# Seven products of halves for x w1 and x w2 of the last two chunk indices, in an RWKV and multiplicative feed-forward kernel

## The chip, the core and the metric

The kernel runs on one core of a Trainium2 chip. The metric is the device time of one launch in microseconds (us). Four runs of the kernel before gave a median of 510.1 us (509.72 to 511.49).

The core has engines that each run their own list of instructions in order and wait for each other by semaphores: PE (matmuls, with weight loads beside them), DVE (vector), ACT (scalar, mostly copies here), POOL (used only in the setup) and SP, which issues the DMA transfers. Matmul results land in PSUM[...]. ACT and DVE carry them on to SBUF.

## What is computed

```python
def _attn_ref(r, k, v, w, u):             # B, H, S, D = 4, 8, 768, 48
    state = zeros((B, H, D, D))
    for t in range(S):
        cur = einsum('bhd,bhe->bhde', u[None] * kt, vt)
        y[:, :, t] = einsum('bhd,bhde->bhe', rt, state + cur)
        state = w[None, :, :, None] * state + einsum('bhd,bhe->bhde', kt, vt)
...
x = attn_out.transpose(0, 2, 1, 3).reshape(B * S, H * D)      # 3072 x 384
a = x @ w1                                # 384 x 1024
b = x @ w2
h = a * b @ w3                            # 1024 x 1024
return h @ w_out                          # 1024 x 384
```

All of it is fp32. The kernel multiplies w3 by w_out first, so that the end is (a * b) times one matrix of 1024 x 384, which it calls w34.

## The kernel before

**Visits.** The sequence is cut into 6 chunks of 128 steps, and a visit is one chunk of one batch row, so there are 24 visits, n = 4c + b. A visit makes a 128-column part of `xT[c]`, the transposed x of chunk index c (384 rows in three blocks of 128, by 512 tokens of the four batch rows). Four visits complete one `xT[c]`.

**The order is written out by hand.** `ORDER` is a list of words such as `a.2.3.2`, and `listed()` runs the function of each word in turn. Each engine gets its instructions in the order of the words. A word says nothing of waits: those follow from the buffers. The words that matter here, with their lines:

- a visit: `kk`, `rr`, `v` load k, r and v (L200); `k` scales k and r on DVE (L404); `x` transposes blocks on DVE (L473); `y` writes them to a scratch in DRAM (L477) and `z` reads them back into one of two buffers `tt` (L485), both on SP; `l` copies the k half on ACT (L490); `d`, `e`, `f`, `g` make the diagonal (L413 to L431); `U` (L517) and `A` (L524) are the state and pair products on PE, `i`, `j` (L540, L541) and `m` (L552) take them on DVE; `o`, `p` spread the state on ACT (L549); `S` (L624) and `V` (L638) make the visit's output on PE, and `Y` (L646) copies it into `xT` on ACT. There is one PSUM buffer for U and A, and one for S and V. Visit n+2 uses the same `tt` as visit n, so `z` of visit n+2 waits for S of visit n.
- the wide products: `a.c.j.part` is x w1 for chunk index c and the 128 columns j of w1, as three matmuls of 128x512 (one for each block of 128 rows of x), L664. `c` copies it to SBUF on ACT (L670), `b` is the same with w2, and `u` multiplies both on DVE into `abt[c, j]` (L675). They share two PSUM banks (tag `f`).
- the last product: `s` makes sums of quarters of `abt` (L708, L711, DVE); `P.c.m.x` is one of seven products of halves, four matmuls of 128x192 (L721); `E` gathers them (L736 on ACT, L738 to L750 on DVE); `D` stores 128 rows of the output (L754). They use the same two banks `f`.
- the weights: `W` fetches (L219), `M`, `N`, `H`, `L`, `Q` convert (L354 to L369), and `G`, `K`, `F`, `X` make w34.

Before the change the words a, c, b, u run for all six chunk indices. The words for c = 4 begin between visits 20 to 23, and those for c = 5 come after visit 23; P, E and D of c = 4 and 5 are interleaved with them.

Of the kernel before, what the change touches and what calls it, by code (L numbers as in the profile page):

```python
# [8 lines left out]
F32 = mybir.dt.float32  # L9
# [13 lines left out]
kk.2 rr.2 v.2 d.0 W.2 N.0 e.0 f.0 M.0 k.0 g.0 H.0 U.0 kk.3 rr.3 d.1 T.0 k.1 L.0 R.0 e.1 kk.4 rr.4 t.0 i.0 f.1 r.0 T.1  # L23
W.3 Q.0 p.0 A.0 M.1 h.1 j.0 S.0 t.1 d.2 R.1 k.2 m.0 r.1 R.2 kk.5 rr.5 e.2 U.1 N.1 r.2 f.2 A.1 M.2 H.1 T.2 i.1 L.1 m.1
V.0 d.3 p.1 W.4 Q.1 v.3 Y.0 t.2 j.1 S.1 g.2 N.2 A.2 k.3 V.1 H.2 R.3 kk.6 rr.6 Y.1 U.2 m.2 M.3 v.4 T.3 N.3 L.2 a.0.0.0
k.4 r.3 W.5 i.2 a.0.1.0 H.3 p.2 c.0.0.0 e.3 L.3 R.4 j.2 S.2 f.3 M.4 W.6 U.3 Q.3 b.0.0.0 o.4 h.3 c.0.1.0 i.3 t.3 V.2
d.4 p.3 k.5 kk.7 rr.7 T.4 Y.2 e.4 A.3 v.5 r.4 x.5 S.3 t.4 b.0.1.0 m.3 o.5 y.5 j.3 M.5 V.3 u.0.0.0 u.0.1.0 U.4 f.4 Y.3
v.6 A.4 Q.2 g.4 a.0.0.1 k.6 N.5 b.0.0.1 M.6 N.6 m.4 c.0.0.1 H.6 a.0.1.1 z.5 u.0.0.1 L.6 H.5 b.0.1.1 c.0.1.1 x.6 W.9
L.5 a.0.2.2 u.0.1.1 y.6 i.4 W.8 l.5 Q.6 p.4 d.5 a.0.3.2 Q.5 c.0.2.2 kk.8 rr.8 j.4 N.4 e.5 S.4 H.4 c.0.3.2 M.8 z.6 U.5
f.5 M.9 V.4 N.8 d.6 L.4 A.5 i.5 kk.9 rr.9 b.0.2.2 Y.4 h.5 o.6 e.6 W.7 p.5 m.5 v.7 l.6 Q.4 b.0.3.2 j.5 u.0.2.2 N.9 k.7  # L30
U.6 f.6 A.6 x.7 g.6 S.5 k.8 y.7 V.5 d.7 M.7 a.0.4.2 m.6 v.8 kk.10 rr.10 o.7 e.7 u.0.3.2 Y.5 f.7 z.7 x.8 b.0.4.2
c.0.4.2 d.8 y.8 h.7 kk.11 rr.11 e.8 i.6 a.0.5.2 f.8 p.6 u.0.4.2 l.7 d.9 j.6 b.0.5.2 c.0.5.2 e.9 H.8 f.9 L.8 H.9 W.11
d.10 L.9 A.7 Q.8 W.12 U.7 u.0.5.2 a.0.6.2 N.7 i.7 H.7 p.7 k.9 L.7 a.0.7.2 j.7 kk.12 rr.12 c.0.6.2 x.9 W.10 Q.9 y.9 S.6
Q.7 c.0.7.2 z.8 o.8 V.6 m.7 e.10 b.0.6.2 Y.6 g.8 v.9 N.10 N.11 S.7 M.10 f.10 M.11 u.0.6.2 z.9 V.7 o.9 H.10 b.0.7.2 l.8
d.11 Y.7 H.11 v.10 L.10 e.11 L.11 Q.10 W.13 g.9 Q.11 W.14 a.1.0.2 N.12 u.0.7.2 M.12 f.11 H.12 M.13 a.1.1.2 d.12 L.12
N.13 e.12 c.1.0.2 W.15 Q.12 M.14 H.13 N.14 L.13 b.1.0.2 H.14 c.1.1.2 W.16 Q.13 L.14 Q.14 W.17 M.15 N.15 b.1.1.2 H.15
u.1.0.2 L.15 Q.15 W.18 M.16 N.16 A.8 H.16 u.1.1.2 a.1.2.2 L.16 m.8 l.9 W.19 N.17 M.17 Q.16 H.17 M.18 b.1.2.2 N.18
c.1.2.2 H.18 L.17 L.18 Q.17 W.20 M.19 Q.18 W.21 G.0.0 N.19 G.0.1 K.0.0 u.1.2.2 U.8 H.19 a.1.3.2 K.0.1 i.8 L.19 k.10
p.8 W.22 M.20 N.20 kk.13 rr.13 x.10 F.0 c.1.3.2 H.20 M.21 y.10 j.8 L.20 Q.19 W.23 M.22 Q.20 N.21 N.22 H.21 H.22 L.21
b.1.3.2 X.0 Q.21 W.24 L.22 Q.22 W.25 M.23 N.23 A.9 u.1.3.2 U.9 H.23 S.8 i.9 L.23 z.10 V.8 k.11 o.10 a.1.4.2 g.10 N.24  # L40
x.11 v.11 kk.14 rr.14 Q.23 Y.8 m.9 y.11 b.1.4.2 p.9 W.26 N.25 f.12 c.1.4.2 j.9 l.10 d.13 e.13 S.9 u.1.4.2 o.11 A.10
z.11 a.1.5.2 m.10 a.1.6.2 c.1.5.2 l.11 a.1.7.2 c.1.6.2 b.1.5.2 V.9 u.1.5.2 U.10 c.1.7.2 v.12 G.1.0 i.10 Y.9 G.1.1 g.11
k.12 b.1.6.2 x.12 kk.15 rr.15 p.10 f.13 y.12 K.1.0 d.14 b.1.7.2 M.24 j.10 M.25 e.14 u.1.6.2 K.1.1 H.24 S.10 H.25 L.24
z.12 A.11 u.1.7.2 o.12 U.11 Q.24 L.25 V.10 m.11 W.28 G.2.0 k.13 g.12 W.27 G.2.1 v.13 F.1 i.11 kk.16 rr.16 Q.25 p.11
f.14 N.26 Y.10 j.11 l.12 d.15 K.2.0 x.13 K.2.1 e.15 y.13 N.27 G.3.0 X.1 U.12 S.11 k.14 o.13 V.11 i.12 kk.17 rr.17 A.12
Y.11 x.14 G.3.1 v.14 g.13 a.2.0.2 z.13 m.12 K.3.0 f.15 y.14 p.12 d.16 G.4.0 K.3.1 e.16 b.2.0.2 j.12 K.4.0 c.2.0.2 l.13
U.13 u.2.0.2 S.12 k.15 z.14 o.14 V.12 i.13 A.13 Y.12 x.15 G.4.1 g.14 v.15 F.2 m.13 y.15 kk.18 rr.18 K.4.1 f.16 l.14
d.17 M.26 e.17 M.27 H.26 p.13 H.27 L.26 j.13 S.13 L.27 W.29 Q.26 M.28 W.30 V.13 Q.27 o.15 z.15 N.28 A.14 Y.13 H.28
U.14 X.2 m.14 G.5.0 L.28 v.16 G.5.1 i.14 g.15 F.3 W.31 Q.28 N.29 k.16 M.29 f.17 kk.19 rr.19 p.14 H.29 j.14 L.29 x.16
l.15 Q.29 S.14 y.16 K.5.0 N.30 d.18 X.3 F.4 K.5.1 N.31 e.18 o.16 z.16 G.6.0 X.4 G.6.1 K.6.0 F.5 M.30 K.6.1 H.30 M.31  # L50
L.30 H.31 Q.30 L.31 s.1.2.0 Q.31 s.1.2.1 F.6 s.1.0.0 X.5 s.1.2.3 s.1.1.0 s.1.3.0 s.1.1.2 s.1.3.1 s.1.1.1 s.1.3.3
s.1.3.2 s.1.0.1 s.1.0.2 s.1.0.3 s.1.2.2 G.7.0 X.6 s.1.1.3 U.15 K.7.0 G.7.1 i.15 P.0.0.0 K.7.1 k.17 p.15 F.7 x.17 kk.20
rr.20 j.15 y.17 A.15 X.7 s.0.1.0 V.14 s.0.0.0 E.0.0.0 l.16 B.0 P.0.1.0 Y.14 v.17 s.0.0.1 g.16 m.15 a.2.1.2 s.0.0.3 B.1
E.0.1.0 f.18 B.2 a.2.2.2 c.2.1.2 B.3 s.0.1.2 s.0.0.2 s.0.2.0 b.2.1.2 d.19 c.2.2.2 s.0.2.2 s.0.2.1 s.0.1.1 s.0.2.3
s.0.3.0 b.2.2.2 s.0.1.3 s.0.3.1 u.2.1.2 s.0.3.3 e.19 s.0.3.2 P.0.0.2 u.2.2.2 P.0.1.2 E.0.0.2 P.0.0.3 E.0.1.2 P.0.0.4
E.0.0.3 P.0.1.3 E.0.0.4 P.0.0.5 E.0.1.3 P.0.1.5 E.0.0.6 E.0.0.5 D.0.0.0 P.0.1.4 E.0.1.6 A.16 E.0.1.4 U.16 E.0.1.5 m.16
D.0.1.0 P.0.0.6 i.16 k.18 p.16 P.0.0.1 j.16 kk.21 rr.21 S.15 x.18 z.17 o.17 V.15 E.0.0.1 E.0.0.7 U.17 Y.15 a.2.3.2
i.17 g.17 y.18 v.18 k.19 D.0.0.1 kk.22 rr.22 p.17 f.19 a.2.4.2 l.17 d.20 j.17 c.2.3.2 x.19 e.20 y.19 P.0.1.1 c.2.4.2
P.0.1.6 E.0.1.1 P.1.0.0 E.0.1.7 D.0.1.1 P.1.0.2 E.1.0.0 P.1.0.3 E.1.0.2 P.1.0.4 E.1.0.3 P.1.0.5 E.1.0.4 P.1.1.0
E.1.0.6 E.1.0.5 D.1.0.0 P.1.0.1 E.1.1.0 P.1.0.6 E.1.0.1 P.1.1.1 E.1.0.7 D.1.0.1 P.1.1.2 E.1.1.1 P.1.1.3 E.1.1.2  # L60
P.1.1.4 E.1.1.3 b.2.3.2 E.1.1.4 b.2.4.2 u.2.3.2 P.2.0.0 u.2.4.2 s.2.0.0 P.1.1.5 s.2.0.2 E.2.0.0 s.2.0.1 s.2.0.3
P.2.1.0 E.1.1.5 E.1.1.6 D.1.1.0 P.1.1.6 A.17 E.1.1.7 S.16 D.1.1.1 E.2.1.0 m.17 z.18 o.18 V.16 U.18 g.18 a.2.5.2 i.18
v.19 k.20 p.18 f.20 kk.23 rr.23 x.20 l.18 a.2.6.2 c.2.5.2 j.18 y.20 d.21 e.21 b.2.5.2 c.2.6.2 a.2.7.2 u.2.5.2 s.2.1.0
s.2.1.2 s.2.1.1 s.2.1.3 b.2.6.2 c.2.7.2 b.2.7.2 u.2.6.2 s.2.2.0 s.2.2.1 s.2.2.2 s.2.2.3 a.3.0.2 Y.16 u.2.7.2 s.2.3.0
s.2.3.1 s.2.3.2 s.2.3.3 b.3.0.2 c.3.0.2 P.2.1.2 u.3.0.2 P.2.0.1 E.2.1.2 P.2.0.2 E.2.0.1 P.2.0.3 E.2.0.2 P.2.0.4
E.2.0.3 P.2.0.5 E.2.0.4 P.2.0.6 E.2.0.5 E.2.0.6 D.2.0.0 P.2.1.3 E.2.0.7 D.2.0.1 P.2.1.4 E.2.1.3 P.2.1.5 E.2.1.4
P.2.1.1 E.2.1.5 E.2.1.6 D.2.1.0 a.3.1.2 E.2.1.1 b.3.1.2 c.3.1.2 P.2.1.6 u.3.1.2 a.3.2.2 E.2.1.7 D.2.1.1 b.3.2.2
c.3.2.2 S.17 u.3.2.2 z.19 o.19 V.17 A.18 Y.17 a.3.3.2 g.19 m.18 v.20 l.19 f.21 b.3.3.2 d.22 c.3.3.2 e.22 A.19 u.3.3.2
U.19 m.19 S.18 i.19 z.20 o.20 V.18 k.21 p.19 a.3.4.2 x.21 g.20 v.21 j.19 y.21 Y.18 P.3.0.0 f.22 l.20 d.23 c.3.4.2 U.20
e.23 E.3.0.0 A.20 i.20 b.3.4.2 k.22 p.20 m.20 x.22 U.21 a.3.5.2 u.3.4.2 y.22 k.23 s.3.0.0 s.3.0.2 s.3.0.1 b.3.5.2  # L70
# [22 lines left out]
def kernel(  # L93
    ctx: ExitStack,
    tc: tile.TileContext,
    r: bass.AP,
    k: bass.AP,
    v: bass.AP,
    w: bass.AP,
    u: bass.AP,  # L100
    moe_w1: bass.AP,
    moe_w2: bass.AP,
    moe_w3: bass.AP,
    moe_w_out: bass.AP,
    out: bass.AP,
):

# [28 lines left out]
    Q = 32  # L147
# [740 lines left out]
```

## Time and profile before

One execution was profiled. It took 513.74 us, its span in the trace is 512.0 us, and 1.7 us lie around the span.

| engine | busy, us | share of the span | instructions |
|---|---|---|---|
| PE (matmul) | 494.3 | 97% | 5222 |
| PE weight loads, beside the matmuls | 325.5 | 64% | 5222 |
| DVE | 277.8 | 54% | 587 |
| ACT | 183.0 | 36% | 456 |
| POOL | 6.0 | 1% | 23 |

The profile's views used below are: the busy times of each engine, for the span or for stretches of it (windows); groups of instructions with busy time, mean time of one, and the idle time before them with what ended it; the waits of one engine; the chain of work that ended last; and the timeline. An fp32 matmul stands in the trace as two instructions, one after the other, so the 138 + 138 matmuls of 128x512 at L664 are counted as 276 + 276. "Mean ns of one" includes what overlaps with the next matmul; the busy time divided by the count is what one adds to PE.

### The profile page before, as it was taken

Reading aid. Unit: us, or ns where it says so; the run is one execution under the profiler, and the core shown is the slowest. Engines: PE = TensorE matmul, PEld = TensorE weight load, DVE = VectorE, ACT = ScalarE, POOL = GpSimd, SP = SyncE. Lnnn points to the kernel's source line nnn. Section 1 sums busy time; section 2 is a strip of 40 time slices with the busy share of each in tenths; the row PEclk is TensorE's granted clock in tenths of the full one; section 3 lists DMA queues with packets and bytes.
Section 4 is the critical chain, followed back from the end, with each engine's and each line's share of the span. In section 5 each row is a group of like instructions: output and inputs, shape, how many; then the busy total and the mean of one; then the engine's idle time right before and its main releaser. Section 6 shows DMA issues by size and latency. Waiting matters only on the chain.

```text
span 512.0 us, 12255 instructions
## 1 busy us (share of the span) xinstructions
PE 494.3 (97%) x5222; PEld 325.5 (64%) x5222; DVE 277.8 (54%) x587; ACT 183.0 (36%) x456; POOL 6.0 (1%) x23
## 2 busy tenths in 40 slices
PE   5689999999999999999999999999999999999996
PEld 5577555355466766678887487564965654855486
DVE  6989998789286767756325432285322215221342
ACT  4676556576277764303103200341061410001000
POOL 4000000000000000000000000000000000000000
PEclk8889999999999999999999999999999999999999
DMA  8898886668448680304402201230060100000001
GB/s 206 192 235 244 237 214 194 180 222 247 130 110 229 172 231 13 78 0 118 116 32 76 65 0 47 63 109 2 1 167 4 49 1 1 15 15 17 1 18 66
DMA packets 96864, 52.72 MB, mean 103 GB/s; under 512 B 77729, under 2 KB 88225, under 8 KB 96801
## 3 DMA queue, kind: packets, MB, share of 16 engines
q1 hardware_dynamic: 96592, 51.85, 37.0%
q8 instruction: 43, 0.70, 0.6%
q14 instruction: 21, 0.16, 0.1%
q10 hardware_dynamic: 208, 0.00, 0.0%
HBM read 39.65 MB, written 12.19 MB: 101 GB/s over the span
## 4 chain that ended last, share of the span: by engine, by line
PE 85%; DMA 6%; DVE 4%; SPq 2%; ACT 1%; issue 1%; ACTq 0%; DVEq 0%
PE ps_b L664 22%; PE ps_a L664 21%; PE ps_w L392 7%; PE ps_y L624 3%; PE ps_y L638 3%; PE ps_s4b L721 3%; PE ps_a12b L721 3%; PE ps_a22t L721 3%; PE ps_s2t L721 3%; PE ps_s1t L721 3%; PE ps_s3t L721 3%; PE ps_a11b L721 3%; PE ps_a L524 3%; PE ps_a L517 2%; DMA raw<-in_moe_w_dram 2%; DMA tt<-scratch 1%
## 5 line engine op out<-in xcount | busy, mean ns | idle before, releaser
L664 PE MATMUL ps_b<-xT,w 128*128 128x512 f32 (+1 forms) x300 | 131.1, 578 | 1.2 <-ACT a L670 1.1
L664 PE MATMUL ps_a<-xT,w 128*128 128x512 f32 (+1 forms) x300 | 131.4, 581 | 0.0
L664 PEld LDWEIGHTS ps_b<-xT,w 128*128 128x128 f32 x300 | 56.0, 190 | 63.9 <-issue 56.7
L675 DVE TENSOR_TENSOR abt<-ps_b,a 128x512 f32<-128x512 f32 (+1 forms) x50 | 33.3, 667 | 111.3 <-PE ps_b L664 111.3
L664 PEld LDWEIGHTS ps_a<-xT,w 128*128 128x128 f32 x300 | 55.3, 190 | 56.9 <-issue 53.6
L670 ACT COPY a<-ps_a 128x512 f32<-128x512 f32 (+1 forms) x50 | 28.2, 567 | 129.3 <-PE ps_a L664 125.4
L549 ACT COPY wide<-st 64x192 f32<-64x192 f32 x88 | 30.6, 348 | 56.0 <-PE ps_y L624 28.1
L431 ACT ACTIVATE AT<-same,dg 128x64 f32<-128x64 f32 x160 | 40.4, 335 | 6.4 <-DVE dg L420 3.9
L392 PE MATMUL ps_w<-wo,w3T 128*128 128x384 f32 x128 | 42.5, 487 | 0.0
L392 PEld LDWEIGHTS ps_w<-wo,w3T 128*128 128x128 f32 x128 | 23.9, 190 | 15.7 <-ACT wide L549 0.2
L366 ACT ACTIVATE t<-raw 128x512 uint32<-128x512 uint32 (+2 forms) x32 | 22.5, 708 | 7.5 <-DVE w3n L362 4.9
L624 PEld LDWEIGHTS ps_y<-tt,wide 128*32 128x32 f32 x1056 | 15.9, 110 | 11.6 <-issue 8.4
L404 DVE TENSOR_TENSOR krs<-krin,pn_in 128x768 f32<-128x768 f32 x24 | 22.7, 948 | 0.0
L624 PE MATMUL ps_y<-tt,wide 128*32 128x64 f32 x1056 | 19.7, 221 | 2.8 <-ACT xT L646 2.8
L638 PE MATMUL ps_y<-AT,vnat 64*64 64x64 f32 x1152 | 22.4, 223 | 0.0
L517 PE MATMUL ps_a<-vnat,krs 64*64 64x48 f32 x704 | 16.7, 227 | 5.8 <-DVE krs L404 4.1
L638 PEld LDWEIGHTS ps_y<-AT,vnat 64*64 64x64 f32 x1152 | 19.3, 136 | 3.0 <-issue 1.3
L552 DVE COPY_PREDICATED AT<-later,ps_a 128x512 f32<-128x512 int32 x24 | 17.4, 726 | 6.8 <-PE ps_a L524 3.7
L473 DVE STREAM_TRANSPOSE tr<-krs 128x768 f32<-128x768 f32 x19 | 18.5, 973 | 4.5 <-DMA scratch<-tr 4.3
L517 PEld LDWEIGHTS ps_a<-vnat,krs 64*64 64x64 f32 x704 | 14.4, 142 | 9.8 <-issue 9.4
L490 ACT COPY kT<-tt 128x512 f32<-128x512 f32 x19 | 11.7, 618 | 20.8 <-DMA tt<-scratch 19.7
L359 DVE TENSOR_SCALAR t<-raw 128x512 uint32<-128x512 uint32 (+2 forms) x32 | 13.9, 437 | 9.4 <-DMA raw<-in_moe_w_dram 5.0
(108 smaller groups left out, 572.3 us busy)
## 6 DMA issues: line engine op xcount, KB each, us to landing
raw<-in_moe_w_dram SPq DMA_DIRECT2D x16, 512.0 KB, 5.0
scratch<-tr SPq DMA_DIRECT2D x19, 384.0 KB, 3.6
raw<-in_moe_w_dram SPq DMA_DIRECT2D x8, 768.0 KB, 6.3
tt<-scratch SPq DMA_DIRECT2D x38, 128.0 KB, 3.2
krin<-in_k_dram SPq DMA_DIRECT2D x24, 192.0 KB, 4.1
krin<-in_r_dram SPq DMA_DIRECT2D x24, 192.0 KB, 4.4
vnat<-in_v_dram SPq DMA_DIRECT2D x24, 192.0 KB, 4.0
raw<-in_moe_w_out_dram SPq DMA_DIRECT2D x8, 384.0 KB, 4.2
```

What stands on the lines that cost most here:

```text
L366: nc.scalar.activation(out=part["t", i], in_=words(i)[0], func=COPY, scale=2.0 ** -29)
L392: nc.tensor.matmul(ps, lhsT=w3T[j][:, kc, :], rhs=wo[kc], start=(kc == 0), stop=(kc == KF - 1))
L404: nc.vector.tensor_mul(krs[n % NS][:, which, :, :D], kr[:, which], pn[:, which, :, :D])
L431: nc.scalar.activation(out=AT[n][:, i, p, :], in_=same, func=COPY, scale=dg[n][:, h:h + 1])
L517: nc.tensor.matmul(added(n)[rows(i), a, p, :], lhsT=kk[rows(a), 2 * p + i, :], rhs=vnat[n % NV][rows(a), 2 * p + i, 0:D], start=True, stop ...
L549: nc.scalar.copy(out=wide[a][n % 2][rows(i), :, i * D:(i + 1) * D], in_=st[units[n][1]][rows(i)])
L624: nc.tensor.matmul(yt[n][g * Q:(g + 1) * Q, a, q, :], lhsT=wide[a][n % 2][:, p, j * Q:(j + 1) * Q], rhs=rw[:, p, 2 * a:2 * a + 2] if fast ...
L638: nc.tensor.matmul(yt[n][rows(g), a, q, :], lhsT=vv[rows(a), x:x + PAD], rhs=AT[n][rows(a), h % 2, h // 2, :], start=(a, g) not in seen, s ...
L664: nc.tensor.matmul(ps, lhsT=(w1 if x == "a" else w2)[:, z, q, js], rhs=xT[c][:, q, ts], start=(q == 0), stop=(q == KM - 1))
L670: nc.scalar.copy(out=a, in_=ps)
L675: nc.vector.tensor_mul(abt[c, j][:, parts_of_tokens[part]], factor["b", c, j, part], factor["sa", c, j, part])
L721: nc.tensor.matmul(ps, lhsT=of[:, m * C:(m + 1) * C], rhs=w34[:, KH * (x == 1) + j, :DH] if x < 2 else made[b][:, j, :], start=(j == 0), s ...
```

## The change

The words a, c, b, u of c = 4 and c = 5 (16 + 16 products of three matmuls) are gone. In their place both chunk indices are done together. Take the first two blocks of 128 rows of x as a 2 x 2 arrangement (row block by chunk index) and the same rows of w1 as 2 x 2 (row block by left or right half of the columns). For each j in 0..3, which gives columns j and j + 4, the four results are made from seven products of one matmul each, with sums of blocks made beforehand, and the third row block is added by four ordinary matmuls into the banks of four of the products.

New words: `wa`, `wb` make sums of w1 and w2 (three new 128x512 tiles each, and one in place), `xs` the sums of x (three new, one in place), `pa`, `pb` are the products, `ga`, `gb` gather them (the first on ACT, seven on DVE for each j and matrix), and `mu` multiplies (four for each j, DVE, SBUF only). `pa`, `pb` take their PSUM in turn from the two banks `f` and the two banks `t`, which visits no longer use by then. The bank of product 4 is read once (ga.4) and then gets one more matmul (`x == 6`) before it is read again (ga.6). The sums of w1 lie in a staging buffer of the weights, those of x in `krin`, and the gathered `a` in `krs` and `vnat`: buffers of the visits and the fetches that are free by then.

All visits now come ahead of the combined products, but for `pa.0.0`, which stands ahead of `U.23`. Words of c = 2, 3 and P, E, D of c = 1 to 3 stand between visits 16 to 23 in another order than before. Early words move a little too: `b.0.0.0` goes ahead of `U.3`, `b.0.1.0` ahead of `S.3`, `T.2` ahead of `U.1`, `t.2` ahead of `L.1`, `p.1` and `Y.0`, `v.3` ahead of `W.4`, `Q.2` ahead of `j.2`. `kr` is `kk` and `rr` in one word.

```diff
 ORDER = """
-U.1 N.1 r.2 f.2 A.1 M.2 H.1 T.2 i.1 L.1 m.1
-V.0 d.3 p.1 W.4 Q.1 v.3 Y.0 t.2 j.1 S.1
+T.2 e.2 r.2 U.1 N.1 f.2 A.1 M.2 H.1 V.0 t.2 i.1 L.1 m.1 v.3 d.3 p.1
+W.4 Q.1 Y.0 j.1 g.2 S.1
...
+P.2.1.3 S.17 E.2.1.3 E.2.1.1 z.19 o.19 V.17 P.2.1.4 i.19 g.19 v.20
+P.2.1.5 E.2.1.4 p.19 f.21 P.2.1.6 y.21 l.19 d.22 j.19 Y.17 A.19 e.22 E.2.1.5 S.18
...
+Y.20 u.3.7.2 U.23 wb.2 S.21 s.3.3.0 ga.0.0 z.23 V.21 s.3.2.3 o.23 s.3.3.1 P.3.0.1 s.3.3.2 g.23 s.3.3.3 i.23
+P.3.0.2 E.3.0.1 p.23 P.3.0.3 l.23 E.3.0.2 Y.21 A.23 E.3.0.3 S.22
...
+Y.23 xs.0 P.3.1.3 E.3.0.7 xs.1 D.3.0.1 P.3.1.4 xs.2 E.3.1.3 xs.3 pa.0.1
...
+pb.1.4 mu.1.0 gb.1.3 pb.1.5 gb.1.4 pb.1.6 gb.1.5 pb.1.7 mu.1.1 gb.1.6
+s.4.1.0 pa.2.0 mu.1.2 s.4.1.1 pa.2.1 ga.2.0 gb.1.7 pa.2.2 s.4.1.2 ga.2.1 mu.1.3 pa.2.3 s.4.1.3 s.5.1.0 pa.2.4 ga.2.2
+s.5.1.1 pa.2.5 s.5.1.2 ga.2.4 s.5.1.3 ga.2.3 pa.2.6 ga.2.5 pa.2.7 ga.2.6 pb.2.0
...
+        def sums_of_w(w, x):
+            a11, a12, a21, a22 = (wide_of[w][:, z * HZ:(z + 1) * HZ, q, :] for z in range(2) for q in range(2))
...
+            s1, s2, s4 = made["w", w]
+            if x == 0:
+                nc.vector.tensor_add(s1, a21, a22)
+            else:
+                out, of, less = ((s2, s1, a11), (a21, a11, a21), (s4, a12, s2))[x - 1]
+                nc.vector.tensor_sub(out, of, less)
...
+        def sums_of_x(x):
+            (b11, b12, b21, b22), (t2, t3, t4) = halves_of_x()
+            out, of, less = ((t3, b22, b12), (b12, b12, b11), (t2, b22, b12), (t4, b21, t2))[x]
+            nc.vector.tensor_sub(out, of, less)
...
+        def product_pair(w, j, x):
+            if x == 6:
+                ps = made["ps", w, j, 4]
+            else:
+                pool, tag = ((psF, "f"), (psT, "t"))[banks[0] % 2]
+                banks[0] += 1
+                ps = pool.tile([P, NT], F32, tag=tag, name=f"ps_{w}{x}_{j}")
+                of_w, of_x = operands(w, j, x)
+                nc.tensor.matmul(ps, lhsT=of_w, rhs=of_x, start=True, stop=x not in (2, 5, 7))
+            made["ps", w, j, x] = ps
+            if x in (2, 5, 6, 7):
+                half, c = {2: (0, 0), 5: (1, 0), 6: (1, 1), 7: (0, 1)}[x]
+                nc.tensor.matmul(ps, lhsT=column(w, j, 2, half), rhs=xT[last[c]][:, 2, :], start=False, stop=True,
+                                 skip_group_check=x == 6)
...
+        def gather_pair(w, j, x):
...
+            if x == 0:
+                nc.scalar.copy(out=t[0], in_=ps)
+            else:
+                out, of = ((1, 0), (0, 0), (2, 1), (3, 1), (1, 2), (2, 2), (3, 3))[x - 1]
+                nc.vector.tensor_add(t[out], ps, t[of])
+
+        def multiply_pair(j, x):
+            b = abt[((last[0], j), (last[0], KH + j), (last[1], KH + j), (last[1], j))[x]]
+            nc.vector.tensor_mul(b, b, made["sa", j % 2][x])
```

## The prediction

> **What bounds the kernel now.** First the page's busy times, then the windows, to see whether the share is an average over unlike stages.
>
> ```profile
> PE 494.3 (97%) x5222; PEld 325.5 (64%) x5222; DVE 277.8 (54%) x587; ACT 183.0 (36%) x456; POOL 6.0 (1%) x23
> ```
>
> ```profile
> 24.00:26.00 2.00, 0.29 (x21) 0.33 (x24) 1.80 (x4) 1.95 (x5) 0.00 (x0) 1.00 0.78 140
> 26.00:28.00 2.00, 2.00 (x100) 1.79 (x89) 2.00 (x4) 1.98 (x9) 0.00 (x0) 0.77 0.83 233
> 28.00:30.00 2.00, 2.00 (x37) 1.58 (x37) 0.45 (x1) 0.45 (x2) 0.00 (x0) 0.50 1.14 300
> ...
> 400.00:425.00 25.00, 25.00 (x303) 14.82 (x302) 4.67 (x10) 5.72 (x12) 0.00 (x0) 1.00 0.03 10
> 425.00:450.00 25.00, 25.00 (x99) 16.86 (x98) 9.95 (x24) 1.76 (x3) 0.00 (x0) 1.00 0.03 12
> 450.00:475.00 25.00, 25.00 (x75) 13.22 (x74) 4.10 (x8) 2.34 (x4) 0.00 (x0) 1.00 0.04 13
> ```
>
> Columns after the stretch: busy PE, weight loads, DVE, ACT, POOL, then the granted PE clock, DMA share, GB/s. From 400 us on PE has no idle time and DVE is busy 4 to 10 of 25 us. So the end is set by PE's work, and a microsecond taken from PE there is a microsecond of the span as long as nobody makes PE wait. The remaining idle time of PE (512.0 - 494.3 = 17.7 us) lies in the first 50 us (10.9 by the 25 us windows), behind the last matmul (512.0 - 507.95 = 4.05), and in short gaps (2.7 together). Which waits end it, by the view of PE's waits:
>
> ```profile
> PE ps_y L624 <- ACT xT L646: 2.8, 1, 2.8
> PE ps_a L517 <- DVE w L369: 1.5, 1, 1.5
> ```
>
> What one instruction costs, by the groups with shapes kept apart:
>
> ```profile
> L664 PE MATMUL ps_a<-xT,w 128*128 128x512 f32 x276 | 125.6, 598 | 0.0
> L664 PE MATMUL ps_b<-xT,w 128*128 128x512 f32 x276 | 125.1, 595 | 1.2 <-ACT a L670 1.1
> L675 DVE TENSOR_TENSOR abt<-ps_b,a 128x512 f32<-128x512 f32 x46 | 31.6, 688 | 110.9 <-PE ps_b L664 110.8
> L711 DVE TENSOR_TENSOR abt<-abt 128x256 f32<-128x256 f32 x24 | 10.0, 420 | 0.3
> ```
>
> The trace counts an fp32 matmul twice. The timeline shows such instructions every 0.429 us (12 in 5.15 us by the chain), so a 128x512 matmul costs PE **0.858 us** (the group's 125.6/276 x 2 = 0.91 holds the ends of products that overlap with other work: I take the steady 0.858).
>
> **The work on PE.** For each j of 0..3 and each matrix, c = 4 and 5 take 2 x 2 x 3 = 12 such matmuls before. After, seven products of one and four of the third block: 11. So 8 x 1 = 8 matmuls go: 8 x 0.858 = **-6.86 us**. Everything else on PE is the same work in another order. Weight loads change with each matmul as before (190 ns each, beside 429 ns of matmul).
>
> **The new work on DVE and ACT.** Per j: gathers 14 (PSUM with SBUF, as L675, 0.69), multiplications 4 (SBUF only; L711's 256 columns take 0.42, and 384 columns at L413 0.55, so 512 by the same slope 0.68), and the 8 sums of s.4, s.5 that were there before (0.42). That is 18 x 0.69 + 8 x 0.42 = 15.8 us of DVE, beside 22 x 0.858 = **18.9 us of PE**. ACT has 2 copies of 0.58. So PE stays the slower one, by 3.1 us in each of four rounds. But the products hold only four banks, so I walked one round. With a matrix's first product at 0, PE starts product 4 at 4.29, 5 at 5.15, the late matmul of bank 4 (x = 6) at 6.86, 7 at 7.72, the next matrix at 9.44; a result reaches DVE 0.21 after PE moves on (a matmul's mean of 0.595 less 0.429, and 0.04 to start). For w2, mu.0 stands between gb.2 and gb.3: gb.2 3.64 to 4.33, mu.0 to 5.04, gb.3 to 5.75, gb.4 5.77 to 6.46; PE wants it at 6.86, **slack 0.4**. The tightest place is the next w1, where DVE still owes mu, gb.7 and sums: counted at full durations, ga.4 ends at 16.48 where PE wants it at 16.30, 0.2 late, in three rounds: 0.6.
>
> Here a rule speaks against the change. The row first: in the timeline the sums of 0.42 us that do not depend on each other start 0.34 apart (476.87, 477.21, 477.54), so about 0.08 of each is hidden. The Trainium skill, "VectorE: DVE Perf Modes", section "The DRAIN you can't avoid", says that the next operation does not start until the pipeline has emptied: then nothing overlaps, and the 0.6 us are paid. By the row some five sums ahead of ga.4 give 0.4 back and nothing is paid. I take the value between, nearer the row: **+0.2**, and keep 0 and 0.6.
>
> The sums `wa`, `wb` (8 x 0.69 = 5.5 us of DVE) stand mostly between P.0 products around 262 us; there DVE frees a bank of P: after wb.0 and wb.1, E.0.0.3 comes 4.5 us after P.0.0.2's end where PE wants the bank at 4.6, so hidden with 0.1 to spare. The four `xs` follow Y.23: V.23's end + 0.6 for Y, then three of 0.69 and E.3.0.7 of 0.36 until pa.0.1 may start, 3.1 us; P.3.0.6, P.3.1.3, P.3.1.4 cover 3 x 1.30 = 3.9. Hidden; without that cover 3.1 us would show once.
>
> **Visits with less cover.** Before, `a.4.0` to `a.4.3` with their b (8 x 2.58 = 20.6 us of PE) filled PE between visits 20 and 23. Now visits must be done with c = 2, 3 and P.1 to P.3 as the filling. Each visit has one long trip: S frees a buffer `tt`, z (four DMAs on SP), `l` on ACT, then A of the visit after next. The timeline shows one, with the columns start, duration, engine:
>
> ```profile
> 333.10 0.88 PE L624 MATMUL ps_y<-tt,wide 128*32 128x64 f32 x48
> ...
> 334.08 2.70 SPq L485 DMA_DIRECT2D tt<-scratch  x4
> ...
> 339.06 0.62 ACT L490 COPY kT<-tt 128x512 f32<-128x512 f32 x1 [1.29 <-DMA tt<-scratch]
> ...
> 339.73 0.79 PE L524 MATMUL ps_a<-tt,kT 64*64 64x64 f32 x32 [0.22 <-ACT kT L490]
> ```
>
> From S's end (333.98) to A: 5.75 us; the same from 276.56, 325.37 and 374.65 gives 5.8, 5.45, 5.55: **5.6**. In the new order PE has between S.17 and A.19: V (0.86) and three P (3.90) = 4.76; the same between S.21 and A.23; between S.15 and A.17: V and four P = 6.06, z there behind one store on SP (0.3); between S.18 and A.20: V, U (0.60), a.3.2 (2.58), S (0.81), V, in the chain's steps, 5.7 to 6.0; the others have over 8. So A.19 and A.23 wait 0.84 each: **+1.7**. What stands behind A on PE is S.18 and S.22, which need Y.17 and Y.21, copied by ACT right after `l`, thus no later. From below this is 0 (a trip of 4.76, which the landings of 2.4 to 3.9 us into `tt` after 260 us just allow), from above see the rivals.
>
> **The early moves.** U.3 waits 1.47 us (35.79) in the second row of the waits. DVE had nothing to finish for it; its v.3 was issued at 30.25 behind W.4, which held SP for 4 us. Now v.3 is ahead of W.4, and b.0.0.0 (1.4 us) ahead of U.3: -1.5. Against this, t.2 (0.59 on ACT) now stands ahead of L.1, p.1 and Y.0, which S.1 awaits (first row of the waits): +0.6. Sum **-0.9**, from 0 (if Q.2, 0.95 us more on DVE ahead of j.2, delays visit 3) to -1.5. PE has hardly a gap from there on, so it is kept to the end.
>
> A second rule bears on this place. The row: PE idles 2.80 us up to 25.70, and 2 us later the granted clock is 0.77, then 0.50 (windows above). The Trainium skill, "TensorE: Matmul & The Clock Gate", Part 1, has the clock fall to half after an idle window of about 3.4 us, whose start is free. The move makes this idle 3.4 us. By the rule a second window may fall: 3.4 us at half speed, 1.7 us lost. By the row the fall is already paid with 2.8 us of idle. I take 0, and keep 1.7 for the range.
>
> **Edits with one answer.** `kr` issues the same two DMAs as kk and rr. The end is alike: last P, 0.36 us of DVE, 3.6 us of store. Its D.5.1.0 comes earlier by one product, which could give 0.1. At 246.3 and 97.3 the gaps of 0.8 and 1.1 (a bank held by `a` until ACT has copied it) keep their order and stay.
>
> **Sum.** -6.86 + 0.2 + 1.7 - 0.9 = **-5.9 us**. The profiled execution would go from 513.74 (span 512.0) to 507.9 (span 506.1); the median of the runs shown lies 3.6 below that execution, and from it the same difference gives 510.1 - 5.9 = **504.2**.
>
> **Rivals.**
> 1. *Everything is hidden.* Trips short or covered, the early gain full: -6.86 - 1.5 = -8.4, 501.7. For it: after 325 us the DMA share is 0.03 to 0.34, and trips could be shorter than at 334. Against it: 5.45 was the shortest of four. Chance 0.17.
> 2. *Hand-overs cost more than walked*: DVE misses PE by 0.2 to 0.4 in each of the eight matrix passes, or the clock falls a second time: -5.9 + 1.7 to 3 = 506 to 507. For it: slack of 0.4 and less, where all waits are new. Against it: DVE is 84% loaded, and a late PE gives DVE time to recover. Chance 0.14.
> 3. *Slower: the trips are exposed.* With trips of T us, A.19 and A.23 wait T - 4.76 each, A.17 and A.20 about T - 6.0 each. The gain is eaten from T = 7.3 (2 x 2.5 + 2 x 1.3 = 7.6); at T = 8 it is 10.5, at most 513. For it: transfers of the scratch took up to 6.5 us to land before 260 us (median 3.5). Against it: after 260 us those into `tt` took 2.4 to 3.9 (median 3.0), and the two late trips are 5.75 and 5.55. Chance 0.05.
> 4. *No difference*: the product saved does not shorten PE because every product of one matmul now waits for its own bank, some 0.08 us each over 88 matmuls (7 us). Against it: P's products change bank every 1.30 us for eight instructions of 0.1625, with nothing between. Chance 0.04.
>
> My forecast, with 503 to 505.6, has 0.60. The range that leaves no more than 2 in 10 out is **501.9 to 507.3**. The measurement tells 0.3% (1.5 us) from no change: faster than 508.6 holds cases 1 and 2 and the forecast, 0.91; same 0.05; slower 0.04.
>
> **What would show it.** In the changed kernel: PE's instructions of 128x512 from 552 to 536 (360 of the old kind and 176 of the new products), one every 0.429 us; rounds of 18.9 us, PE idle under 1 us in them, DVE at 0.8; waits of PE on ACT's `l` (kT) of 0.5 to 1.2 us twice; no wait at U.3; one of about 3.4 us at S.1. Wrong it would be if PE waits for the gathers (`krs`, `vnat`, `abt` as releasers) by more than 2 us in all, or on kT by more than 3.

## The result and the profile after

The changed kernel takes 507.72 us (median of 34 runs, 505.32 to 510.65), the kernel before 510.11 in the same rounds (55 runs, 506.89 to 513.81). The ratio is 0.9949, with a 95% interval of 0.9936 to 0.9961: **2.6 us less** (2.0 to 3.3), where 5.9 were forecast. The profiled execution took 508.31 (span 506.5), 5.4 less than that of before, which had been a long one for its kernel (513.74 beside a median of 510.11). So a comparison of these two executions alone would have flattered the forecast.

The page's busy times and, below them, four stretches by engine (busy PE, weight loads, DVE, ACT, POOL, then granted PE clock, DMA share, GB/s):

```profile
PE 486.3 (96%) x5206; PEld 321.3 (63%) x5206; DVE 318.0 (63%) x655; ACT 178.4 (35%) x448; POOL 6.0 (1%) x23
```

```profile
28.00:30.00 2.00, 1.57 (x40) 1.11 (x38) 0.98 (x3) 0.80 (x1) 0.00 (x0) 1.00 0.76 158
...
406.00:425.00 19.00, 19.00 (x45) 8.36 (x44) 14.35 (x27) 1.17 (x2) 0.00 (x0) 1.00 0.00 0
425.00:444.00 19.00, 19.00 (x46) 8.38 (x45) 14.37 (x26) 1.17 (x2) 0.00 (x0) 1.00 0.01 1
444.00:463.00 19.00, 19.00 (x46) 8.48 (x45) 14.42 (x26) 1.17 (x2) 0.00 (x0) 1.00 0.00 0
```

The rounds of combined products leave PE no idle time at all, with DVE busy 14.4 of 19 us (0.76). The groups with shapes kept apart show the work that went:

```profile
L670 PE MATMUL ps_b<-xT,w 128*128 128x512 f32 x180 | 81.8, 596 | 0.3 <-ACT a L676 0.3
L670 PE MATMUL ps_a<-xT,w 128*128 128x512 f32 x180 | 81.4, 596 | 0.0
...
L825 PE MATMUL ps_b<-xT,w 128*128 128x512 f32 x32 | 16.3, 592 | 0.0
L829 PE MATMUL ps_b<-xT,w 128*128 128x512 f32 x32 | 15.9, 592 | 0.0
```

360 instructions of the old kind are left, and the new lines L825 and L829 (two of their eight groups are shown) hold 176: 536 in all, as counted. None of the eight new groups waits. So the missing 3.3 us are not there. The waits of PE (us in total, times, longest) say where to look:

```profile
PE ps_a L670 <- ACT xT L652: 2.6, 2, 1.6
PE ps_y L644 <- issue: 2.2, 2, 1.7
...
PE ps_y L630 <- ACT xT L652: 0.7, 1, 0.7
PE ps_a L670 <- ACT a L676: 0.6, 1, 0.6
PE ps_a L530 <- ACT kT L496: 0.6, 1, 0.6
PE ps_s2t L727 <- DVE osb_top L744: 0.6, 1, 0.6
...
PE ps_s3t L727 <- DVE u L746: 0.5, 1, 0.5
```

The wait at U.3 is gone, and S.1 waits 0.7 us for `xT`, where about 3.4 were forecast. New are 2.6 us of x w1 on `xT` (a.0.0.0 and a.0.0.1), 0.6 on `a` (a.0.1.1), 2.2 on nothing that this view names ("issue", in the middle of V.0 and V.1; the last section says on what), all before 48 us, and later 0.6 at A.19 and 1.0 at P.1.0.2 and P.1.0.3. The timeline names what stands ahead of `xT` (start, duration, engine; what ended the idle time is in brackets):

```profile
41.65 0.92 ACT L360 ACTIVATE w<-raw 128x768 f32<-128x768 f32 x1 [1.91 <-DMA raw<-in_moe_w_dram]
...
42.46 0.70 ACT L555 COPY wide<-st 64x192 f32<-64x192 f32 x2
...
43.18 0.48 ACT L652 COPY xT<-ps_y 128x384 f32<-128x384 f32 x1
43.72 0.48 PE L670 MATMUL ps_a<-xT,w 128*128 128x256 f32 x1 [1.64 <-ACT xT L652]
```

V.3 had ended on PE by 41.2. Its copy Y.3 is short and ready to go, but in ACT's queue M.5 stands ahead of it, and M.5 waits for weights that land at 41.6. PE wanted a.0.0.1 at 42.1 and got it at 43.7.

### The profile page after: what moved, and what is told of

It is laid out like the page before. It is cut to its first block, busy times and chain, and to the rows that moved or that the text cites. A ratio compares the mean times of both kernels' runs of the same rounds, so it can differ in the third digit from the quotient of the medians.

```text
span 506.5 us, 12288 instructions
## 1 busy us (share of the span) xinstructions
PE 486.3 (96%) x5206; PEld 321.3 (63%) x5206; DVE 318.0 (63%) x655; ACT 178.4 (35%) x448; POOL 6.0 (1%) x23
## 4 chain that ended last, share of the span: by engine, by line
PE 82%; DMA 9%; ACT 3%; DVE 3%; SPq 1%; issue 1%; ACTq 0%; DVEq 0%
PE ps_b L670 15%; PE ps_a L670 14%; PE ps_w L398 7%; PE ps_b L825 5%; PE ps_a L825 5%; PE ps_s3t L727 3%; PE ps_s2t L727 3%; PE ps_s4b L727 3%; PE ps_a12b L727 3%; PE ps_s1t L727 3%; PE ps_a22t L727 3%; DMA raw<-in_moe_w_dram 3%; PE ps_b L829 3%; PE ps_a L829 3%; PE ps_y L644 3%; PE ps_a11b L727 3%
## 5 line engine op out<-in xcount | busy, mean ns | idle before, releaser
L670 PE MATMUL ps_a<-xT,w 128*128 128x512 f32 (+1 forms) x204 | 87.4, 572 | 3.2 <-ACT xT L652 2.6
L670 PE MATMUL ps_b<-xT,w 128*128 128x512 f32 (+1 forms) x204 | 87.9, 572 | 0.4 <-ACT a L676 0.3
L670 PEld LDWEIGHTS ps_b<-xT,w 128*128 128x128 f32 x204 | 37.8, 190 | 41.1 <-issue 36.4
L670 PEld LDWEIGHTS ps_a<-xT,w 128*128 128x128 f32 x204 | 37.7, 190 | 41.3 <-issue 35.2
L681 DVE TENSOR_TENSOR abt<-ps_b,a 128x512 f32<-128x512 f32 (+1 forms) x34 | 22.2, 657 | 50.7 <-PE ps_b L670 50.5
L676 ACT COPY a<-ps_a 128x512 f32<-128x512 f32 (+1 forms) x34 | 18.9, 557 | 50.0 <-PE ps_a L670 40.3
L850 DVE TENSOR_TENSOR abt<-ps_b,abt 128x512 f32<-128x512 f32 x28 | 18.9, 685 | 12.8 <-PE ps_b L829 8.4
L742 ACT COPY m<-ps_a11b 128x192 f32<-128x192 f32 x12 | 3.8, 315 | 49.4 <-PE ps_a11b L727 49.4
```

The lines of the kernel that those rows point to most:

```text
L670: nc.tensor.matmul(ps, lhsT=(w1 if x == "a" else w2)[:, z, q, js], rhs=xT[c][:, q, ts], start=(q == 0), stop=(q == KM - 1))
```

## The experiments

Times scatter: one kernel's runs spread over up to 7 us, and four kernels that were run a second time gave ratios 0.0017 to 0.0021 apart (0.9 to 1.1 us). So each comparison below is made by ratio to the kernel before in the same rounds, and less than about 1 us between two kernels is not told apart. The ratio is not the quotient of two medians: start_old has a slightly lower median than late_only, from the same rounds, and the higher ratio.

| kernel | median us (runs) | ratio to before, 95% |
|---|---|---|
| changed | 507.72 (34) | 0.9949 [0.9936, 0.9961] |
| before_again (before, unchanged) | 510.98 (22) | 1.0011 [0.9994, 1.0027] |
| early_only | 512.26 (17) | 1.0032 [1.0013, 1.0050] |
| late_only | 506.51 (6) | 0.9918 [0.9889, 0.9947] |
| late_again (the same kernel) | 506.18 (9) | 0.9935 [0.9912, 0.9958] |
| start_old | 506.25 (11) | 0.9946 [0.9922, 0.9969] |
| start_old_again | 507.30 (14) | 0.9928 [0.9905, 0.9951] |
| old_v3_b | 506.93 (16) | 0.9924 [0.9902, 0.9945] |
| old_m_ahead | 507.71 (21) | 0.9940 [0.9924, 0.9956] |
| m_behind | 507.26 (22) | 0.9944 [0.9928, 0.9960] |
| m_old | 507.20 (16) | 0.9950 [0.9930, 0.9970] |
| m_old_again | 507.37 (12) | 0.9929 [0.9900, 0.9959] |
| t2_q2_back | 507.77 (20) | 0.9954 [0.9936, 0.9972] |
| v3_b_back | 507.55 (22) | 0.9951 [0.9936, 0.9966] |
| light_old | 505.25 (6) | 0.9893 [0.9858, 0.9927] |
| light_after | 507.05 (9) | 0.9929 [0.9901, 0.9958] |
| after_covered | 505.24 (6) | 0.9880 [0.9849, 0.9912] |
| late_covered | 504.02 (6) | 0.9873 [0.9839, 0.9908] |
| covered_again (the same kernel) | 503.72 (6) | 0.9856 [0.9826, 0.9887] |

**The change cut in two.** Up to P.0.0.2 both orders hold the same 733 words. So one half of the change can be run without the other.

```diff
 late_only:   the first 733 words as before, the rest as changed
 early_only:  the first 733 words as changed, the rest as before
 start_old:   the first 139 words (to about 43 us) as before, the rest as changed
 before_again: nothing changed
```

> The changed kernel with the first 733 words of the order (all up to P.0.0.2, about 227 us) as they stood before; the combined products and the visits ahead of them stay. Theory A, the missing 3.5 us are lost by the early moves: the later part alone gains the 6.6 us that the two traces show from a.0.2.2 on, 503.0 to 504.3. Theory B, they are lost in the visits and rounds, and the profiled execution was a lucky one: 507 to 508, as with the whole change.

> The kernel before with the first 733 words of the order in the new arrangement and nothing else. Theory A: slower by what is missing, 513 to 514.5. Theory B: 509.2 to 510.2, the -0.9 forecast or nothing.

> The changed kernel with only the first 139 words (to about 43 us: T.2, t.2, v.3 ahead of W.4, b.0.0.0 ahead of U.3, b.0.1.0, Q.2, t.3, r.4, M.5) as before. If the loss comes from these moves: 503 to 504.5. If it comes from the early words after them (W.8/W.9, M and L words): 507 to 508. Theory B: 507 to 508 as well.

> The kernel before, unchanged, for a second profile of it. Theory A: its first 128x512 product (a.0.2.2), at 49.20 us in the first profile with two long spells of the clock at half, starts 2 to 4 us earlier in an execution near the median. Theory B: about 49.2 again. The time is 510.1 by both.

The late part alone gives 3.3 to 4.2 us; with the new early part on top, only 2.6 are left. The early part alone costs 1.6 (1.1 against the unchanged kernel run beside it). Start times of PE's words, read from each profile, put the late part apart from the scatter of the start (us; the last column ends with the last matmul):

| profile | U.0 to a.0.2.2 | a.0.2.2 to P.0.0.2 | P.0.0.2 to the end of PE |
|---|---|---|---|
| before / before_again / early_only | 36.7 / 35.9 / 37.2 | 174.4 / 174.0 / 173.5 | 284.4 / 282.8 / 283.2 |
| late_only / start_old / changed | 35.7 / 36.0 / 37.9 | 174.3 / 173.0 / 173.9 | 279.0 / 278.4 / 278.3 |
| late_covered / covered_again / after_covered | 36.4 / 36.9 / 37.1 | 174.7 / 173.8 / 174.0 | 276.2 / 276.4 / 276.4 |

The late part is 4.5 us shorter (283.4 in the mean of the three old ones, 278.9 in the mean of the fourteen profiles with the changed late part), which is nearly the 5.0 that the forecast gave it (-6.86 + 0.2 + 1.7). So the early part is where the forecast failed. With the first 43 us as before (start_old, twice) the ratio is 0.0003 and 0.0021 below that of the changed kernel: 0.2 and 1.1 us come back. Up to about half of the early loss may lie there; the scatter doesn't tell more.

**The forecast's own step, alone.** The late part with the old start, and only v.3 and the b words moved:

```diff
-W.4 Q.1 v.3 ... U.3 Q.3 b.0.0.0 ... S.3 t.4 b.0.1.0
+v.3 W.4 Q.1 ... b.0.0.0 U.3 Q.3 ... b.0.1.0 S.3 t.4
```

> The new late part with the old early part, in which only v.3 goes ahead of W.4, b.0.0.0 ahead of U.3 and b.0.1.0 ahead of S.3. The prediction's own step (PE has hardly a gap from there on, so the 1.3 to 1.5 us of U.3 are kept to the end): the wait at U.3 goes and the time falls by 1.2, to 505.3. Theory A: the wait at U.3 goes, A.3 starts 1 to 1.5 us earlier relative to S.1, but Y.3 still stands behind M.5, whose weights land where they landed, so 0.7 to 1.2 us come back as a wait at a.0.0.1; the time falls by 0.3, with 0 to 0.7.

The wait at U.3 went, and no gain is seen: 0.9924 stands between the two results of the same kernel without the move (0.9918, 0.9935). With 1 us of scatter the time alone says little; the timeline shows the places to which the wait went:

```profile
37.65 0.66 PE L458 MATMUL ps_kT<-ident,krs 128*128 128x128 f32 x4 [0.99 <-ACT kT L465]
...
41.72 0.96 ACT L361 ACTIVATE w<-raw 128x768 f32<-128x768 f32 x1 [1.16 <-DMA raw<-in_moe_w_dram]
...
42.57 0.47 ACT L653 COPY xT<-ps_y 128x384 f32<-128x384 f32 x1
...
43.09 1.13 PE L671 MATMUL ps_a<-xT,w 128*128 128x256 f32 x4 [0.40 <-ACT xT L653]
```

PE saved the wait at U.3 and stood 0.99 for ACT at T.4, 0.40 at a.0.0.1. M.5 starts at 41.72, as late as in the changed kernel: ACT's work behind that transfer doesn't get earlier when PE does.

**The weight conversions on ACT.** Added alone to the old start, taken away alone from the changed kernel, and put further back than they ever were:

```diff
 old_m_ahead (on late_only):         M.3 ahead of Y.1, M.5 ahead of o.5, M.6 ahead of g.4
 m_old, m_old_again (on changed):    M.3 behind Y.1, M.5 behind o.5, M.6 behind g.4
 m_behind (on changed):              M.3 behind Y.1, M.5 behind Y.3, M.6 behind c.0.0.1
```

> The new late part with the old early part (506.5 us when it ran), in which only M.3 goes ahead of Y.1, M.5 ahead of o.5 and M.6 ahead of g.4, as the change has it. Theory A: waits of PE at a.0.0.0, a.0.0.1 or a.0.1.1 appear that the old early part does not have, together 0.7 to 1.5 us, and the time goes up by as much, to 507.2 to 508. Rival B: no such waits, the time stays within 0.5 of 506.5.

> The changed kernel with ACT's order of the weight conversions as before in three places: M.3 behind Y.1, M.5 right behind o.5, M.6 right behind g.4; all else as changed. If the early loss (1.5 us between the changed kernel and the one with the old early part) comes from these three, the time falls by 0.9 to 1.6 from 507.7 and the waits at a.0.0.0 and a.0.1.1 go; if it comes from the words moved on PE, SP or DVE, it stays within 0.5 of 507.7.

> The changed kernel with M.3 behind Y.1, M.5 behind o.5 and M.6 behind g.4 once more (mean 507.3 of 16 runs the first time, beside 507.9 of the changed kernel). If these three words carry the early loss, the mean of both times together is 506.6 to 507.0; if it stays at 507.3 or above, they carry at most half of it.

> The changed kernel with three words moved back on ACT: M.3 behind Y.1, M.5 behind Y.3, M.6 behind c.0.0.1. Theory A (what the early moves cost is that M.3, M.5 and M.6 wait for weight transfers at the head of ACT's queue while Y.1, Y.3 and c.0.0.1, which PE wants, stand behind them): PE's waits at a.0.0.0, a.0.0.1 and a.0.1.1 (0.95, 1.64 and 0.59 us in the profile of the changed kernel) fall to 0.4 together, and the time from 507.7 to 505 to 506. Rival B (the early stretch is set by other things, such as v's arrival, DVE or the clock, and ACT's order only shows it): other waits take their place before 60 us, and the time stays within 0.7 of 507.7.

Added, they bring the waits at a.0.0.0 (1.04), a.0.0.1 (0.40) and a.0.1.1 (0.28) and 0.3 to 1.1 us of time. Taken away, the waits change places: in m_behind all three are gone, but V.3 waits 0.64 for DVE (m.3) and S.1 2.96 for `xT`; in m_old_again a.0.0.1 still waits 1.26, since Y.3 stands behind M.5 in the old order too. The time falls by 0 and 1.0 in the two runs of one kernel, and by 0.3 in m_behind, where at least 0.9 and 1.7 were expected. Theory A held for the waits and failed for the time.

**The other two groups**, each put back alone in the changed kernel:

```diff
 t2_q2_back: T.2 behind H.1, t.2 behind Y.0, Q.2 behind A.4
 v3_b_back:  v.3 behind W.4, v.5 behind rr.7, b.0.0.0 behind U.3, b.0.1.0 behind S.3
```

> The changed kernel with T.2, t.2 and Q.2 in their old places. If t.2 ahead of L.1, p.1 and Y.0 on ACT, or Q.2 ahead of j.2 on DVE, carry the early loss, the time falls by 0.6 to 1.5 (0.6 is the prediction's own price for t.2); if they cost nothing, as the missing rise of the wait at S.1 suggests, it stays within 0.5 of 507.7.

> The changed kernel with v.3 behind W.4, v.5 behind kk.7 and rr.7, b.0.0.0 behind U.3 and b.0.1.0 behind S.3, as before. By the prediction's step this gives up 1.5 us: the wait at U.3 comes back and the time rises to 509. By the theory that the start is bound by transfers and by ACT behind them, the wait at U.3 comes back, those at a.0.0.1 and a.0.1.1 shrink by as much, and the time stays within 0.5 of 507.7.

Neither moves the time beyond the scatter (0.9954, 0.9951). With v.3 and b back, U.3 waits 0.70 again and the waits at a.0.0.0, a.0.0.1 and a.0.1.1 are gone: the same time in another place, as the second theory said. (The profiled execution was the longest of that kernel, and S.1 waits 3.53 in it.)

**Less to transfer.** Five of the early weight fetches cut to a third of their bytes (those weights are then wrong):

```diff
-            queue.dma_start(out=landed[i], in_=pieces[i])
+            part = slice(0, 1) if i in (4, 5, 6, 8, 9) else slice(0, m)
+            queue.dma_start(out=landed[i][:, part], in_=pieces[i][:, part])
```

> The new late part with the old early part (506.7 us, mean of 15 runs), in which the fetches of pieces 4, 5, 6, 8 and 9 of w1 and w2 move only the first of their three row blocks (256 of 768 KB), so that the weights of these pieces are wrong. Theory C (the start is bound by the transfers): the waits at S.1 and U.3 shrink, PE's stalls without a visible releaser (at the 219th, 346th and 601st matmul) go, and the time falls by 1.5 to 3, to 504 to 505. If DVE and ACT bind the start it falls by less than 0.8.

> The changed kernel with the same five fetches cut to a third (the same weights are wrong). Theory C: the waits at a.0.0.0, a.0.0.1 and a.0.1.1 (0.95, 1.64 and 0.59 us) go, because the conversions on ACT no longer wait for weights; the early moves then bring what was forecast or at least cost nothing, and the time is not above that of the light kernel with the old early part: 503.5 to 505. If the early loss of about 1.2 us has nothing to do with transfers, it stays between the two light kernels.

The waits of PE in the light kernel with the new early part, 24 to 60 us:

```profile
PE ps_y L632 <- ACT xT L654: 2.8, 1, 2.8
PE ps_a L672 <- ACT xT L654: 1.0, 1, 1.0
PE ps_y L646 <- issue: 0.2, 1, 0.2
```

a.0.0.1 and a.0.1.1 no longer wait, as theory C said; a.0.0.0 still does (1.0), against theory C, but M.3's piece was not among the five. U.0 to a.0.2.2 takes 35.1, beside 37.9 in the changed kernel, and 35.4 in light_old. But the two light kernels are 1.8 us apart in time (0.9929 and 0.9893), with the old start ahead (light_old has no wait at U.3 either, and gains 1.3 to 2.1 us on late_only and its repeat); the profiled execution of light_after was one of its shortest. So the transfers make those two waits, and they are not the whole of the early loss.

**Cover for the late waits.** In the changed kernel the bank of a.2.3.2 is freed by c.2.3.2, which stands on ACT behind l.18 (`kT`), and l.18 waits for a scratch transfer:

```profile
254.36 0.62 ACT L496 COPY kT<-tt 128x512 f32<-128x512 f32 x1 [2.61 <-DMA tt<-scratch]
254.73 0.35 DVE L744 TENSOR_TENSOR osb_top<-ps_a12b,m 128x192 f32<-128x192 f32 x1
254.88 0.58 ACT L676 COPY a<-ps_a 128x512 f32<-128x512 f32 x1
255.14 1.57 PE L727 MATMUL ps_s2t<-t,raw 128*128 128x192 f32 x8 [0.56 <-DVE osb_top L744]
...
257.16 1.08 PE L727 MATMUL ps_s3t<-w,abt 128*128 128x192 f32 x5 [0.45 <-DVE u L746]
```

With one bank held, P.1.0.2 and P.1.0.3 follow each other through the other one, and each waits for the gather before it. In the next kernels c.2.3.2 goes ahead of l.18, and S.17 goes one product earlier, so that A.19's trip has 1.3 us more cover:

```diff
-l.18 y.20 j.18 d.21 P.1.0.1 c.2.3.2 ... P.2.1.3 S.17
+c.2.3.2 l.18 y.20 j.18 d.21 P.1.0.1 ... S.17 P.2.1.3
```

> The new late part with the old early part, in which c.2.3.2 goes ahead of l.18 on ACT and S.17 ahead of P.2.1.3. If the waits of PE at P.1.0.2 and P.1.0.3 come from c.2.3.2 standing behind l.18, which waits for a scratch transfer, they go (0.84 and 0.45 us in the profile of that kernel), and A.19's 0.57 goes as its trip is covered by one more product: the time falls by 1.3 to 1.9, to 504.6 to 505.2. Rival: the waits only move (to P.1.0.3 for DVE, or to A.20, whose trip then starts no earlier), and the time falls by less than 0.6.

> The new late part with c.2.3.2 ahead of l.18 and S.17 ahead of P.2.1.3 and the old early part, once more: 504 to 505, faster than the changed kernel and than the one before.

> The changed kernel with c.2.3.2 ahead of l.18 and S.17 ahead of P.2.1.3. The waits at P.1.0.2, P.1.0.3 and A.19 (1.57 us together) go, and the time falls to 505.5 to 506.3; against the same late part with the old early part (504.0) the early loss of 1.2 us should be seen again, 0.5 to 2.

The same place in late_covered:

```profile
252.75 0.58 ACT L677 COPY a<-ps_a 128x512 f32<-128x512 f32 x1 [1.57 <-PE ps_a L671]
...
253.84 0.62 ACT L497 COPY kT<-tt 128x512 f32<-128x512 f32 x1 [0.50 <-DMA tt<-scratch]
...
253.85 1.46 PE L728 MATMUL ps_s2t<-t,raw 128*128 128x192 f32 x8
```

The copy runs while ACT would have waited, and P.1.0.2 starts without a wait. In its profile PE has no wait left from 200 us to the end, and the late part falls from 278.9 to 276.3. With the old early part this is 503.7 to 504.0 us, 6.5 to 7.3 below the kernel before and 3.9 to 4.7 below the changed one: **a version that beats both**. With the new early part it is 0.4 and 1.2 us slower (0.9880 beside 0.9873 and 0.9856): the early loss again, though within the scatter of repeats.

## Why the forecast was wrong

Behind P.0.0.2 PE's busy time fell by 6.1 us (282.9 in the mean of the three old profiles, 276.9 in the fourteen), and its idle time rose by 1.5 (0.5, 2.0): -4.5 together, beside -5.0 in the forecast. The rest of the miss, within the scatter, lies in the early moves.

- **Work on PE, -6.86: right in the count, somewhat too large.** 536 instructions, 0.858 us each product. By start times the 128x512 work behind P.0.0.2 takes 8.0 us less (151.2, 143.2), but P's words take 1.6 more (107.5, 109.1). That everything else on PE is "the same work in another order" holds for the number of instructions and not quite for their time; what sets P's products further apart isn't shown.
- **The rounds, +0.2: 0.** By the timeline the first products of the matrices start 9.44 us apart (399.77, 409.21), and PE never waits in them. The row of overlapping sums was the better guide; by the DRAIN section, read as "nothing overlaps", 0.6 us of waits would have shown. (The section itself, in the Trainium skill's "VectorE: DVE Perf Modes", goes on that an operation which is not held starts earlier; the forecast left that out.)
- **Visits with less cover, +1.7: 0.56.** A.19's trip took 5.5 us, about as estimated (S.17's end at 319.34, A.19 at 324.85); its wait was 0.56 here and 0.25 to 1.08 in the other profiles with the same late words. A.23's trip took 4.5 (370.34 to the end of `kT` at 374.87), shorter than the four from which 5.6 was taken, and PE's filling covered it; A.20 waited 0 to 0.4.
- **Left out: P.1.0.2 and P.1.0.3, +1.0** (0.9 to 1.6 in the others). The walk checked banks in the rounds and around `wa` and `wb`, but not those between the moved visits 18 and 20. c.2.3.2 behind l.18 was to be seen in the order of words.
- **The early moves, -0.9: about +1. This is the step that failed**, in its last sentence: "PE has hardly a gap from there on, so it is kept to the end." The wait at U.3 went as forecast, and A.3 came 1.3 us earlier after U.0 (early_only, 24.9, beside before_again, 26.1). But a.0.0.1, 6 us later, did not: it starts 30.9 us after U.0, beside 30.5, and the longest wait in this row of early_only stands before it:

```profile
PE ps_a L664 <- ACT xT L646: 2.1, 2, 1.5
```

  That PE has no gap behind a wait says only that the others are ahead of it, not by how much. The trace of before, on which the forecast rests, has it on ACT:

```profile
42.16 0.94 ACT L354 ACTIVATE w<-raw 128x768 f32<-128x768 f32 x1 [0.65 <-DMA raw<-in_moe_w_dram]
43.00 0.46 ACT L646 COPY xT<-ps_y 128x384 f32<-128x384 f32 x1
```

  M.5 waits for its weights until 42.16, Y.3 is done at 43.46, and a.0.0.1 starts on PE at 43.72. The lead is 0.26 us, so of 1.47 us saved at U.3 no more than that could pass a.0.0.1. And the moves did not bring M.5 forward: it starts 28.0 to 29.5 us after U.0 in the seven profiles that have v.3 and the b words moved (those with fewer bytes, and m_behind, which moves M.5 back, left out), and 27.8 to 29.7 in seven of the eight with the old start (31.6 in late_again). The gain could not be kept; old_v3_b shows about 0, give or take 1 us, where 1.2 was expected. The further loss of about 1 us was not in the sum at all (1.1, 1.8 and 1.2 us in three pairs of kernels that differ in the early part alone and ran in the same rounds: early_only, the light kernels, the covered ones): M.3 ahead of Y.1 and M.5 ahead of o.5 were moved and neither named among the early moves nor priced. The price +0.6 for t.2 ahead of S.1's wait was wrong too: that wait did not grow (1.71 us in early_only, 2.37 in before_again), and t2_q2_back gave nothing back.
- **The clock, 0: the row was read too surely.** The stretch at half speed at 27 to 30.5 us is absent in the changed kernel (1.00 at 28 us above), although PE idled 1.71 and 0.66 us close together there.

**Open:** which early word carries the further loss. None of the three groups alone brings it back for sure (m_old, t2_q2_back, v3_b_back). The conversions may hold a part of it (old_m_ahead, 0.3 to 1.1 us), and light_after says that transfers are not all of it. About a hundred of the words that change places before P.0.0.2 stand behind the first 139, and of these only M.6 was moved in a run.

## What to carry to other kernels

Before a removed wait is counted as gain, go to the next two or three places where that engine meets another, and ask how early the other one was there: the gain is capped by the smallest of these leads. An instruction that waits for a transfer is also a wait for all that stands behind it on its engine; moved ahead of a copy that a busier engine wants, it makes that copy late (a wait of 1.04 us at a.0.0.0 in old_m_ahead), even if its own result isn't wanted soon. The same question finds gains: a copy that is ready goes ahead of one that waits for a transfer.

## What the hardware showed that was not expected

**PE stalls in the middle of a group, at the same instructions, for a block of its own instructions.** In the changed kernel V.0 stops behind its 5th matmul record and goes on; in late_again V.1 stops behind its 28th:

```profile
21.14 0.28 PE L644 MATMUL ps_y<-AT,vnat 64*64 64x64 f32 x5
23.13 0.91 PE L644 MATMUL ps_y<-AT,vnat 64*64 64x64 f32 x43 [1.71 <-issue]
```

```profile
26.73 1.06 PE L645 MATMUL ps_y<-AT,vnat 64*64 64x64 f32 x28
29.73 0.91 PE L645 MATMUL ps_y<-AT,vnat 64*64 64x64 f32 x20 [1.93 <-issue]
```

Over all 20 profiles there are 21 such stalls, of 0.2 to 1.9 us, in 16 profiles, with the old order and the new. They come only ahead of the matmul records 219, 346 and 601 of the execution, counted from 0 (all before 44 us), and of 2248, once 2247 (160 to 163 us). From 219 to 346 it is 127 matmuls with as many weight loads, 254 instructions, and from 346 to 601 it is 510. The Trainium skill, "Runtime: NRT & Kernel Launch", section "Instruction fetch mechanics", has each engine's instructions come through a DMA queue in blocks of 256, and calls the cost of a boundary mostly hidden. The trace has such a queue:

```profile
q8 instruction: 43, 0.70, 0.6%
```

These are 43 packets of 16,384 bytes each, with a start and a duration for every one. All 21 stalls end 1.2 to 1.5 us after the end of one of them. Where the packet ended more than 1.6 us ahead of a record at which other executions stall, PE didn't stall; at record 473, halfway between 346 and 601, it ended 3.8 us ahead or more in every profile, and none stalls. So PE waited for its own instructions, and here that is not hidden. The DMA share in the 2 to 4 us up to the early stalls was 0.55 to 1.08; what delayed the packets isn't shown. Before 44 us seven of the nine profiles with the new early part (whole, or with one group put back) have such a stall, and two of the eleven with the old one. Whether this is a part of the early loss isn't shown either: in the changed kernel S.1, behind 1.71 us of stall, starts at 24.70, and in the kernel before at 25.70. The stalls change from one execution to the next, so they may be a part of the scatter.

**The half-speed clock after S.1.** In 20 profiles it followed S.1's wait in nine. Where PE idled 2.37 us or more in one piece it fell in seven of eight; below 2.2 us it fell in two of twelve (1.90, and 0.66 with two stalls beside it). The Trainium skill, "TensorE: Matmul & The Clock Gate", Part 1, as used in the forecast, asks for an idle window of about 3.4 us; these runs show the fall with a full microsecond less in one piece. A half-speed stretch lasts 3.41 us in these traces, or two or three times that.
